# A delta-rule attention and gated-experts kernel: its greedy scheduler against a written order of its steps

## The chip, the cores and the metric

The kernel runs on one core of one Trainium2 chip. The metric is the device time of one launch in microseconds (us). Engines are called by the profile's names: PE (matrix multiply; PEld is its weight load), DVE (vector), ACT (scalar), POOL (GpSimd), SP (the queue that issues the DMAs).

## What is computed

Two layers, one after the other. The first is a recurrent attention over 4 batches, 8 heads, 768 tokens and a head width of 48; the second is a mixture of 4 causal-attention experts over the first one's output, 2 experts per token.

```python
k_n = k / (norm(k) + 1e-06)                    # per token
for t in range(S):                             # S = 768
    y[t]  = q[t] @ state                       # state: 48x48 per batch and head
    state = state + beta[t] * outer(k_n[t], v[t] - k_n[t] @ state)
x = y as (B, S, 384)
logits = x @ w_gate; the top 2 of 4 experts; w = softmax over the two
for e in range(4):                             # width 64
    q, k, v = x @ wq[e], x @ wk[e], x @ wv[e]
    a = softmax(causal(q @ k.T / 8))
    out += gate[e] * (a @ v @ wo[e])
```

## The kernel before

**Tiling.** The work is cut into six units n (NU = 6), each 256 tokens of two batches: units 0, 1, 2 are the three pieces of one pair of batches, 3, 4, 5 of the other, so the state starts anew at unit 3. A unit has four chunks c of 64 tokens (CH = 4). Inside a chunk the recurrence is solved as a triangular system, so that the state moves on chunk by chunk.

**Steps.** All work is cut into small functions; each is one step and has a short name with its indices (unit first). Those that the prediction speaks of:

- lg, lq, lc: loads of k, q and of the k/v pair of a chunk (lines 65, 69, 73), issued on SP; w: load of a weight block, with its split into a high and a low part on ACT and POOL (L130 to L132).
- gr, gq: Gram matrices k.k and k.q of a chunk on PE, brought out of PSUM by ACT (gr, L163; for unit 0 with DVE, L165, L166) or masked by DVE (gq, L175).
- si (L179, L182): three transposes on DVE that lay a unit's Gram matrices out for the solve; pre: the norms (DVE) and the scaling before the solve (L229 on DVE for unit 0, L233 on POOL for the others); sv: the 32 steps of the solve, on DVE for unit 0 (with sg, the other part of the columns, on POOL) and on POOL for units 1 to 5 (L244, L242, L258, L261, L262); so, sn (L278, L275): its result transposed back, on DVE; m1, m2: the halves merged on PE, out by ACT (L290, L304); cl (L311): clears on POOL.
- vt (L78, POOL): v scaled by the norms. ks, u, s, q, y: the chain of a chunk, on PE with ACT (L352, L383, L384) and DVE (L346, L364, L385, L386) between; ks of a chunk needs s of the chunk before it. hx (L392): six small DMAs that spread y for the next layer.
- pj, pv: projections to q, k and v of the experts; gt: gates; mx (L501): scores without exp on PE, maxima over them by DVE; mp, mr: the maxima split and turned to rows; sc: scores again with the maximum taken off, exp on ACT (L552 to L555) ; av: times v, out by ACT (L571, L572); nm, ft, fo (L588, L591, L592, L605, L607): scaling, transposes, the product with wo, and the store.

PE products that leave through the pool `pm_` share three PSUM buffers (gr and gq take two at a time), so a step must wait until the engine behind it has emptied the one three places back. The chunk products and av have PSUM of their own.

**Fillers.** `filler()` is a matmul of zeros with 252 columns into an unused part of the tile po (128x252 in the trace). It computes nothing that is used.

**What sets the order.** Each engine works its instructions off in the order in which the program issues them. The kernel finds this order while it is built, by a greedy scheduler: every step is an `Item` with estimated costs on each engine, dependencies by name, and the PSUM pool that it takes. The items stand in 20 lists; of the heads of the lists whose dependencies are issued, the one with the lowest key goes next, the key being the time at which it can start by the scheduler's own clocks plus a hand-tuned offset by kind and unit (`PRI`). Before a PE step it issues fillers as long as its own clock for PE lies more than 0.355 us before the step's start, and more when its window of matmul columns is low:

```python
if it.pe:
    gap = it.start() - CLK["P"]
    if gap < FMAX:
        while it.start() - CLK["P"] > FMIN:
            CLK["P"] = pe_run(CLK["P"], 0.108, 256)
            filler()
    for _ in range(30):
        if ("gr", 0, CH - 1) not in R or not low(it):
            break
        CLK["P"] = pe_run(CLK["P"], 0.108, 256)
        filler()
it.emit()
```

## Time and profile before

| | us |
|---|---|
| median of 3 runs (570.06 to 574.22) | 572.21 |
| the profiled execution's own time | 573.86 |
| its span, first to last instruction | 572.2 |
| PE busy, fillers included | 520.0 |
| DVE, ACT, POOL busy | 314.1, 260.3, 245.3 |
| mean granted PE clock | 0.981 |

The profile is of one execution. A row of a timeline gives the start in us from the span's start, the duration, the engine, the line, what is written<-read, and how many instructions are merged; in square brackets stands how long the engine had been idle before, and what ended that. A row of groups gives busy time and mean ns of one, then the idle time before the group's instructions. PEclk is the share of the full PE clock that was granted. Matmuls are pipelined, so a row's durations overlap with those of the next.

### The profile page before, as it was taken

What the parts mean: (1) busy time and instruction counts of PE and PEld (TensorE: products, weight loads), DVE (VectorE), ACT (ScalarE), POOL (GpSimd) and SP (SyncE); (2) the same over time, 40 slices, a digit from 0 to 9 for tenths busy, and PEclk for the clock granted to TensorE, in tenths of its full rate; (3) what the DMA queues carried; (4) which work ended last, traced back from release to release, by engine and by line L of the source; (5) the groups of instructions that cost most, each with busy time, mean ns of one, the idle gap of its engine ahead of it and who ended that gap; (6) DMA issues with size and microseconds to landing.
All of it is one profiled execution on the core that took longest, in us unless ns stands there. A gap on an engine that the chain in (4) does not pass through costs nothing. (4 is left out here: it accounts for less than half of the span.)

```text
span 572.2 us, 24003 instructions
## 1 busy us (share of the span) xinstructions
PE 520.0 (91%) x10686; PEld 447.3 (78%) x10686; DVE 314.1 (55%) x745; ACT 260.3 (45%) x642; POOL 245.3 (43%) x422
## 2 busy tenths in 40 slices
PE   6996978888988899898899997999999999999997
PEld 4795767777877668797787886988888787887796
DVE  3996842387534483485888052366744645256701
ACT  2821314335625346357213743574256365574263
POOL 4485266760367811038818875200269810000000
PEclk9997998999999999899899999999999999999999
DMA  8400143200153002520001044002220002110001
GB/s 294 176 11 29 40 118 96 62 1 2 50 181 119 4 1 69 155 71 2 15 15 48 5 122 153 11 1 76 54 67 17 29 3 86 23 37 8 22 2 56
DMA packets 19399, 33.36 MB, mean 58 GB/s; under 512 B 2912, under 2 KB 9440, under 8 KB 19296
## 3 DMA queue, kind: packets, MB, share of 16 engines
q1 hardware_dynamic: 19296, 31.83, 17.9%
q8 instruction: 84, 1.38, 1.0%
q14 instruction: 19, 0.16, 0.1%
HBM read 24.74 MB, written 4.72 MB: 51 GB/s over the span
## 5 line engine op out<-in xcount | busy, mean ns | idle before, releaser
L46 PE MATMUL po<-zb 128*128 128x252 bf16 x798 | 112.8, 281 | 5.7 <-ACT rs L572 3.4
L46 PEld LDWEIGHTS <-zb 128*128 128x128 bf16 x798 | 75.7, 101 | 20.8 <-issue 7.3
L242 POOL TENSOR_TENSOR B<-B,tm 128x30 f32<-128x30 f32 (+9 forms) x150 | 79.0, 527 | 11.7
L244 POOL TENSOR_TENSOR tm<-B 128x30 f32<-128x30 f32 (+9 forms) x150 | 72.7, 485 | 10.4
L78 POOL TENSOR_TENSOR kv<-kv,nt 128x384 f32<-128x384 f32 x24 | 20.3, 848 | 83.9 <-DMA kv<-in_kv_dram 50.6
L46 PE MATMUL po<-VS,at 128*64 128x65 f32 x1344 | 51.1, 229 | 0.3 <-issue 0.3
L46 PEld LDWEIGHTS po<-VS,at 128*64 128x64 f32 x1344 | 44.2, 140 | 5.6 <-issue 2.4
L571 ACT ACTIVATE os<-po 128x128 f32<-128x128 f32 x48 | 13.3, 277 | 44.2 <-PE po L46 44.1
L233 POOL TENSOR_TENSOR B<-B,nn 128x1024 f32<-128x1024 f32 x5 | 11.8, 2366 | 48.1 <-PE pm__4351 L46 18.3
L311 POOL MEMSET tt<- 32x1024 f32 x10 | 9.5, 945 | 53.0 <-PE pm__2438 L46 19.2
L46 PE MATMUL py<-qf,sb 48*48 48x64 f32 x704 | 24.5, 221 | 5.6 <-DVE h L386 5.5
L364 DVE TENSOR_TENSOR sb<-sb,xu 112x384 f32<-112x384 f32 x20 | 11.0, 551 | 30.6 <-PE xu L46 21.7
L46 PEld LDWEIGHTS py<-qf,sb 48*48 48x48 f32 x704 | 21.5, 122 | 8.1 <-DVE h L386 7.3
L383 ACT ACTIVATE xh<-py 112x384 fp32r<-112x384 f32 x24 | 11.8, 490 | 32.9 <-PE py L46 32.1
L385 DVE TENSOR_TENSOR xh<-py,xh 112x384 fp32r<-112x384 f32 x24 | 13.4, 557 | 21.4 <-ACT h L384 21.3
L46 PEld LDWEIGHTS <-identb 128*128 128x128 bf16 x192 | 18.5, 97 | 7.4 <-issue 1.4
L346 DVE TENSOR_TENSOR xs<-kv,xu 128x384 f32<-128x384 f32 x22 | 12.1, 551 | 14.5 <-PE xu L46 10.6
L182 DVE STREAM_TRANSPOSE B<-tt 32x1024 f32<-32x1024 f32 x10 | 19.5, 1954 | 0.2
L46 PE MATMUL xu<-xs,tt 64*64 64x48 f32 x768 | 17.2, 225 | 1.6 <-DVE xs L346 1.5
L519 ACT ACTIVATE mp<-mx 128x8 fp32r<-128x8 f32 x12 | 2.5, 208 | 34.8 <-DVE mx L501 17.9
L46 PE MATMUL xu<-sb,kf 48*64 48x48 f32 x704 | 15.6, 223 | 2.8 <-DVE sb L364 2.0
L46 PEld LDWEIGHTS xu<-sb,kf 48*64 48x64 f32 x704 | 12.7, 134 | 6.6 <-DVE sb L364 4.4
(2005 smaller groups left out, 1461.0 us busy)
## 6 DMA issues: line engine op xcount, KB each, us to landing
kv<-in_kv_dram SPq DMA_DIRECT2D x24, 384.0 KB, 3.7
kf<-in_kq_dram SPq DMA_DIRECT2D x24, 256.0 KB, 3.8
qf<-in_kq_dram SPq DMA_DIRECT2D x24, 256.0 KB, 3.3
out_dram<-ot SPq DMA_DIRECT2D x24, 192.0 KB, 1.9
xh<-h SPq DMA_DIRECT2D x72, 32.0 KB, 2.6
VS<-in_kt_dram SPq DMA_DIRECT2D x4, 192.0 KB, 5.0
wst<-in_wqk_dram SPq DMA_DIRECT2D x3, 256.0 KB, 6.0
wst<-in_wvg_dram SPq DMA_DIRECT2D x1, 256.0 KB, 5.9
```

The lines of the kernel that those rows point to most:

```text
L46: T.matmul(o, lhsT=a, rhs=b, start=start, stop=stop, skip_group_check=True)
L78: G.tensor_tensor(vt, vt, PR[n]["nt"][:, c * NP:c * NP + NP, None].to_broadcast([128, NP, HD]), op=OP.mult)
L182: V.transpose(B[r:r + 32], gf[r:r + 32, :, 0:32].rearrange("p t j -> p j t"))
L233: G.tensor_tensor(B, B, bc(nn, 32), op=OP.mult)
L242: e.tensor_tensor(X[:, a:b, i + 1:], X[:, a:b, i + 1:], tv, op=OP.add)
L244: e.tensor_tensor(tv, R[:, :, i + 1:].to_broadcast([128, w, m]), X[:, a:b, i:i + 1].to_broadcast([128, w, m]), op=OP.mult)
L311: G.memset(TG[n % 2][r + 32:r + 64, :, 0:32], 0.0)
L346: V.tensor_tensor(eight(XB), eight(vt), PX, op=OP.subtract)
L364: V.tensor_tensor(eight(new), eight(state(n, c)), SP, op=OP.add)
L383: S.activation(hi, Y[:, :, 0:3], AF.Copy)
L385: V.tensor_tensor(lo, Y[:, :, 0:3], hi, op=OP.subtract)
L571: S.activation(os[:, :, e], O[:, :, 0:EH], AF.Copy)
```

## The change

The scheduler, its items, costs, clocks and offsets are taken out. In their place stand a string ORDER with the names of all steps in the order in which they are issued, and a table DO from each name to its function. A token like `+41` issues that many fillers at that place.

```diff
+ORDER = """
+fr3 +41 gr0.3 sq0 sr0 sq1 sr1 sq2 +8 gr0.0 sq3 sr2 sr3 lq1.1 pre0.0 +4 gr0.1 lg1.3 pre0.1 pre0.2 pre0.3 lg1.1 kc3 fr1
...
++109 gq0.0 so0 +33 gq0.3 +11 m10.0 w0 sn0 m10.1 +3 m20.0 lg2.0 w5 si1 pre1.0 pre1.1 m20.3 u0.0 pre1.2 pre1.3 w2 m20.2
...
+"""
-    PR = {}
+    PR = {n: dict(gf=TG[n % 2], B=LB[n % 2][:, 1:]) for n in range(NU)}
...
-    CLK = dict(P=0.0, A=0.0, V=0.0, G=0.0)
-    BUF = dict(pm=[0.0] * 3, po=[0.0])
...
+    DO = {}
+    def step(kind, fn, *index):
+        DO[kind + ".".join(map(str, index))] = lambda: fn(*index)
+    for k, a in enumerate(WL):
+        step("w", lambda k: load_weights(*WL[k]), k)
...
+    for x in ORDER.split():
+        if x in DO:
+            DO[x]()
+        else:
+            for _ in range(int(x[1:])):
+                filler()
```

The step functions themselves are the same, and so are the counts of every instruction but the fillers: the program before issues 798 of them (one ahead of the scheduler), the changed one 383. Counted up to four places of the program (in both orders the same names): ahead of u0.0, the first product of the chain, 292 before and 298 now; from there to u1.0 142 and 54; from there to the projections of the last unit (pj5) 321 and 16; behind them 43 and 15. The sets of PE steps that lie between these places are almost the same in both: u0.0 has m20.1 behind it now and gq0.3 and m20.3 ahead of it; u1.0 has av0.1.3 and three of the m21 behind it and q1.0 ahead of it; at pj5 they are equal. What changes is the order inside, and which unit's and which batch's steps alternate. Dependencies that the scheduler took as a whole (mx only when all projections of its unit are done) are now as fine as the data: mx0.0.0.0 stands ahead of the second half's projections.

Three places, as the built programs have them. Lines of the changed program are 61 to 62 higher from the step functions on (L278 is L339 there).

DVE at the end of the first solve, before (L261 and L262 are its last step, L278 is so0, L275 sn0):

```order
L242 TENSOR_TENSOR B_122<-B_122,tm 128x4
L242 TENSOR_TENSOR B_122<-B_122,tm 128x5
L261 TENSOR_TENSOR B_122<-B_122,aa 128x288
L262 COPY B_122<-aa 128x9
L278 STREAM_TRANSPOSE tt_109<-B_122 128x32x32
L275 STREAM_TRANSPOSE tn<-B_122 128x32x32
```

and changed (L236 is the masking of gq):

```order
L303 TENSOR_TENSOR B_122<-B_122,tm 128x4
L303 TENSOR_TENSOR B_122<-B_122,tm 128x5
L322 TENSOR_TENSOR B_122<-B_122,aa 128x288
L323 COPY B_122<-aa 128x9
L236 TENSOR_TENSOR pm<-pm__873,cst 128x256
L236 TENSOR_TENSOR pm<-pm__874,cst 128x256
L339 STREAM_TRANSPOSE tt_109<-B_122 128x32x32
L236 TENSOR_TENSOR pm<-pm__928,cst 128x256
L236 TENSOR_TENSOR pm<-pm__929,cst 128x256
L336 STREAM_TRANSPOSE tn<-B_122 128x32x32
```

Three of the four gq0 steps are done ahead of, or within, so0 and sn0 now (one more pair stands a few rows higher); before they came behind.

DVE at the maxima of unit 2, before (L592 is ft, L179 and L182 are si4, L501 the maxima of batch 0):

```order
L592 TENSOR_TENSOR ol<-pm__4731,oh 128x512
L179 STREAM_TRANSPOSE B_122<-tt_109 128x1024
L182 STREAM_TRANSPOSE B_122<-tt_109 32x1024 x2
L501 TENSOR_REDUCE mx<-pm__4811 128x1
L501 TENSOR_REDUCE mx<-pm__4814 128x1
L501 TENSOR_REDUCE mx<-pm__4817 128x1
L501 TENSOR_REDUCE mx<-pm__4860 128x1
```

and changed (L564 maxima, L582 mp, L593 mr, L511 pv, L240 and L243 si4):

```order
L564 TENSOR_REDUCE mx<-pm__4558 128x1
L582 TENSOR_TENSOR mp<-mx,mp 128x2x4
L236 TENSOR_TENSOR pm<-pm__4566,cst 128x256
L236 TENSOR_TENSOR pm<-pm__4567,cst 128x256
L593 CAST QL<-pm__4586 8x2x256
L564 TENSOR_REDUCE mx<-pm__4593 128x1
L511 COPY lg<-pm__4600 128x4
L240 STREAM_TRANSPOSE B_122<-tt_109 128x1024
L243 STREAM_TRANSPOSE B_122<-tt_109 32x1024 x2
```

The three transposes of si4 stood ahead of the maxima of batch 0; they stand behind them and behind mr2.0 now, where PE goes on with scores that ACT empties.

PE in the last unit, before (three-digit sizes: 128x512 is a full mx product, woh and wol belong to fo):

```order
L46 MATMUL pm__8845<-woh,ol 128x384 x2
L46 MATMUL pm__8855<-KA,QA 128x512
L46 MATMUL pm__8858<-KA,QA 128x512
L46 MATMUL pm__8861<-KA,QA 128x512
L46 MATMUL pm__8864<-KA,QA 128x512
L46 LDWEIGHTS zb
L46 MATMUL po<-zb 128x252
L46 MATMUL pm__8869<-KA,QA 128x128
```

and changed (KA, QA 128x512 is mx; pairs QA, KA and QL, KH are a score):

```order
L109 MATMUL pm__8470<-QL,KH 128x256
L109 MATMUL pm__8476<-KA,QA 128x512
L109 MATMUL pm__8480<-QA,KA 128x256
L109 MATMUL pm__8480<-QL,KH 128x256
L109 MATMUL pm__8480<-QA,KA 128x256
L109 MATMUL pm__8480<-QL,KH 128x256
L109 MATMUL pm__8487<-QA,KA 128x256
L109 MATMUL pm__8487<-QL,KH 128x256
L109 MATMUL pm__8487<-QA,KA 128x256
L109 MATMUL pm__8487<-QL,KH 128x256
L109 MATMUL pm__8493<-KA,QA 128x512
L109 MATMUL po<-VS,at 64x65 x22
```

Where maxima of batch 1 followed one another with fillers between, scores and av of batch 0 stand between them now.

## Prediction

> **What bounds the kernel now.** I read the page first. PE is busy nearly all the time, the other engines about half of it:

> ```profile
> PE 520.0 (91%) x10686; PEld 447.3 (78%) x10686; DVE 314.1 (55%) x745; ACT 260.3 (45%) x642; POOL 245.3 (43%) x422
> PEclk9997998999999999899899999999999999999999
> ```

> But 520.0 us of PE holds the fillers, which compute nothing. So I cut the span at three places that both programs pass in the same state: 63.3 us (u0.0), 149.7 us (u1.0) and 499.7 us (first projection of unit 5). The windows view gives each stretch its length and then PE's busy time:

> ```profile
> 0.00:63.30 63.30, 53.18 (x996) 42.70 (x996) 47.52 (x159) 22.29 (x46) 37.28 (x69) 0.95 0.36 124
> 63.30:149.70 86.40, 75.78 (x1808) 65.02 (x1806) 48.21 (x120) 33.89 (x90) 42.34 (x72) 0.98 0.17 47
> 149.70:499.70 350.00, 323.53 (x7103) 281.00 (x7102) 187.81 (x394) 168.73 (x417) 165.69 (x282) 0.99 0.19 56
> 499.70:572.20 72.50, 67.55 (x786) 58.54 (x783) 30.53 (x73) 35.35 (x91) 0.00 (x0) 0.99 0.08 26
> ```

> and the groups view, asked for the same four windows, the fillers' row in each (count, busy us, mean ns):

> ```profile
> L46 PE MATMUL po<-zb 128*128 128x252 bf16 x292 | 38.7, 297 | 1.1 <-DVE zb L51 1.1
> L46 PE MATMUL po<-zb 128*128 128x252 bf16 x142 | 19.8, 272 | 2.4 <-ACT rs L572 1.8 <-issue 0.6
> L46 PE MATMUL po<-zb 128*128 128x252 bf16 x322 | 47.0, 273 | 1.9 <-ACT rs L572 1.3 <-DVE ol L592 0.4 <-issue 0.2
> L46 PE MATMUL po<-zb 128*128 128x252 bf16 x43 | 7.5, 274 | 0.3 <-ACT rs L572 0.3
> ```

> Busy less fillers is PE's own work: 14.5, 56.0, 276.5 and 60.0 us. The rest of each stretch is lost to PE, by filler or idle: 48.8, 30.4, 73.5 and 12.5 us, 165.2 in all. DVE, the next engine, has 187.8 of 350 us in the longest stretch. So PE's own work and what it waits for between set the time. A filler is not by itself a gain to be had, though: where PE filled while it had to wait, taking the filler out leaves the wait.

> **Stretch 1, up to u0.0.** The first solve on DVE sets it. The timeline of all engines:

> ```profile
> 21.34 1.30 DVE L229 SCALAR_TENSOR_TENSOR B<-B,aa 128x736 f32<-128x736 f32 x2
> 45.43 1.43 POOL L270 TENSOR_TENSOR B<-VS,aa 128x736 f32<-128x736 f32 x1 [1.64 <-DVE B L242]
> 45.52 1.65 DVE L261 TENSOR_TENSOR B<-B,aa 128x288 f32<-128x288 f32 x1
> 48.58 1.95 DVE L278 STREAM_TRANSPOSE tt<-B 128x1024 f32<-128x1024 f32 x1
> 50.44 1.90 DVE L275 STREAM_TRANSPOSE tn<-B 128x1024 f32<-128x1024 f32 x1
> 50.68 1.92 PE L46 MATMUL pm__872<-tt 32*32 32x32 f32 x64 [4.48 <-DVE tt L278]
> 52.53 2.70 PE L46 MATMUL po<-zb 128*128 128x252 bf16 x12
> 55.16 1.44 PE L46 MATMUL pm__919<-tt 32*32 32x32 f32 x64
> 57.26 0.42 DVE L175 TENSOR_TENSOR pm<-pm__955,cst 128x256 f32<-128x256 f32 x1 [4.92 <-PE pm__956 L46]
> 57.93 1.99 DVE L179 STREAM_TRANSPOSE B<-tt 128x1024 f32<-128x1024 f32 x1
> 63.31 0.68 PE L46 MATMUL xu<-xs,tt 64*64 64x48 f32 x32
> ```

> PE has run through all the fillers ahead of m10.0 and stands idle 4.48 us more; the merge begins 0.15 us after so0 has ended (48.58 + 1.95 = 50.53). That end moves by two edits. Two pairs of gq maskings stand ahead of so0 now, each 0.67 us by the start of the next instruction (57.26 to 57.93): +1.4. Ahead of L229 the written order has the Gram matrices as steps of the same kind and count, with fewer fillers between (8, 4, 6 against 6, 6, 12), so that DVE should come to it a little sooner; the trace has no row for that, so I bound it by nothing and by 2 us and take 1. POOL gets a weight split and a vt between its steps, and had 1.64 us to spare at its end; I add nothing.

> From so0 to u0.0 the old order needs 63.31 - 50.53 = 12.8 us: m10.0, 12 fillers, m10.1, two gq with 7 fillers between, m20.0, 12 fillers, m20.1. The new one has m10.0, m10.1, 3 fillers, m20.0, m20.3 and then u0.0, where m20.0 waits for sn0, which is behind one more gq pair: 0.67 + 1.90 = 2.6 us after so0. Behind that come m20.0, its eviction by ACT (0.60 us, the L304 row below) and m20.3. An m2 of unit 0 has 64 products as m10.1 has (1.44 us up to the end of the last); I take 1.2 each, and 5.6 us in all. Sum: 1.4 - 1 + (5.6 - 12.8) = **-6.8 us**, between -9 and -2: u0.0 at 56.5.

> **Stretch 2, u0.0 to u1.0.** One unit alone is in flight, and two chains run: chunk by chunk on PE, ACT and DVE, and the solve of unit 1 on POOL. In time:

> ```profile
> 59.85 0.60 ACT L304 ACTIVATE tt<-pm__1014 128x512 f32<-128x512 f32 x1 [1.05 <-issue]
> 59.96 3.90 DVE L182 STREAM_TRANSPOSE B<-tt 32x1024 f32<-32x1024 f32 x2
> 72.59 2.35 POOL L233 TENSOR_TENSOR B<-B,nn 128x1024 f32<-128x1024 f32 x1 [1.54 <-DVE nn L232]
> 125.59 0.24 POOL L262 COPY B<-aa 128x32 f32<-128x32 f32 x1
> 132.25 1.98 DVE L179 STREAM_TRANSPOSE B<-tt 128x1024 f32<-128x1024 f32 x1 [1.67 <-ACT tt L163]
> 138.17 1.99 DVE L278 STREAM_TRANSPOSE tt<-B 128x1024 f32<-128x1024 f32 x1
> 149.72 0.68 PE L46 MATMUL xu<-xs,tt 64*64 64x48 f32 x32
> ```

> and POOL's groups between 74.9 and 138 us:

> ```profile
> L242 POOL TENSOR_TENSOR B<-B,tm 128x30 f32<-128x30 f32 (+14 forms) x30 | 15.5, 516 | 2.3
> L78 POOL TENSOR_TENSOR kv<-kv,nt 128x384 f32<-128x384 f32 x4 | 3.3, 828 | 9.7 <-DMA kv<-in_kv_dram 4.6 <-DVE h L386 2.8 <-DVE pm L175 1.7
> ```

> The solve takes POOL from 74.9 to 125.8 us, 50.9, of which four vt cost 3.3 and the wait ahead of them 9.7. Then so1 waits another 12.3 us, since si2 stands ahead of it on DVE and itself waits for the last Gram matrix of unit 2. In the new order si1 begins right behind sn0, at about 53.5 instead of 57.9 us, so POOL may start at 70.5; vt1.1 stands behind the solve, and if 3 of the 9.7 us are left, the solve takes 50.9 - 6.7 - 0.8 = 43.4 and ends at 114. The two Gram matrices of unit 2 are issued earlier, so I give so1 4 us behind that, and keep the old 11.6 us from so1 to u1.0: 129.5 against u0.0 at 56.5, a stretch of 73 us. PE alone could do its 56.0 plus 54 fillers of 0.14 us (7.6) in 64. I take 72: **-14 us**, between -22 (PE without a wait) and -3 (si2 as late as before).

> **Stretch 3, u1.0 to the last projections.** 322 fillers become 16. What they cover shows where DVE is kept by a transpose:

> ```profile
> 282.73 3.97 DVE L182 STREAM_TRANSPOSE B<-tt 32x1024 f32<-32x1024 f32 x2
> 285.69 3.83 PE L46 MATMUL po<-zb 128*128 128x252 bf16 x34
> 286.73 0.69 DVE L501 TENSOR_REDUCE mx<-pm__4811 128x1 f32<-128x512 f32 x1
> 396.28 3.91 DVE L182 STREAM_TRANSPOSE B<-tt 32x1024 f32<-32x1024 f32 x2
> 397.57 3.50 PE L46 MATMUL po<-zb 128*128 128x252 bf16 x31
> ```

> Three mx products fill the three PSUM buffers, DVE comes to the first one only when si4 is done at 286.7, and PE fills 3.8 us; the same behind si5. These are waits: without the fillers and in the old order they would stay. The new order puts si4 behind the maxima of its batch and scores (emptied by ACT) behind si4, so PE has work there. Likewise a maximum holds DVE 0.69 us, while its PE product is shorter; rows of maxima that followed each other have scores between them now. Short waits inside the chain (ks, u, s with ACT or DVE between) keep their length, and only more of other units' work between them hides them. Of 73.5 us lost I take half as left, 37; 16 fillers add 2.3 us (47.0 / 322 each). For the clock I add 5 us, three more pieces as below. 276.5 + 37 + 2.3 + 5 = 320.8: **-29 us**. If only the fillers go that cover nothing, it is some -5; if a quarter of the loss is left, -53.

> **The clock.** Fillers also keep PE busy. After the start the trace has four pieces of 3.4 us at half clock. Windows of that length around two of them (third from the end is the granted clock):

> ```profile
> 86.50:89.91 3.41, 1.83 (x62) 1.30 (x62) 0.56 (x1) 0.49 (x1) 1.81 (x4) 1.00 0.23 48
> 89.91:93.33 3.42, 3.30 (x15) 3.31 (x16) 0.76 (x2) 0.28 (x1) 0.19 (x1) 0.50 0.79 264
> 236.69:240.10 3.41, 2.14 (x59) 1.63 (x53) 1.18 (x4) 1.80 (x5) 0.00 (x0) 1.00 0.50 125
> 240.10:243.51 3.41, 3.41 (x112) 3.41 (x111) 3.38 (x2) 0.49 (x1) 0.00 (x0) 0.50 0.74 249
> ```

> A window in which PE was busy 1.83 or 2.14 of 3.41 us was followed by one at half clock, so a piece costs at most half its length, 1.7 us, and comes when some 1.3 us of a window is idle. The new order can have more such windows where a wait is bare now.

> [...]

> **Stretch 4, the end.** 43 fillers become 15, 13 of them at the same place as before, ahead of fo5.1.0:

> ```profile
> 565.21 1.45 PE L46 MATMUL po<-zb 128*128 128x252 bf16 x12
> ```

> That wait for the last ft stays. Of the 12.5 us lost, maxima run beside scores now; I keep 7: **-5.5 us**, between -8 and -1.

> **The sum.** -6.8 - 14 - 29.2 - 5.5 = -55.5 us against the profiled execution's own 573.86 us gives 518.4. Its median stands 1.65 us lower (572.21), so I predict 517 us. All lower bounds together (-9, -22, -53, -8) give 480, all upper ones (-2, -3, -5, -1) 561.

> **Rivals.** (a) The waits stay: the fillers only marked them, and what the new order puts there comes due elsewhere. For it: PE idles 4.48 us at so0 although it filled, and the 34 and 31 fillers above ended with DVE's transpose. Against it: the order puts ready work at just these places. Stretch 1 as forecast, and little else (-6.8, -5, -12, -2; 517 + 30): 547 us. (b) The order fills nearly all: a quarter of the third stretch's loss is left, the others at their lower ends: 480 us, as above. For it: DVE, ACT and POOL are busy only about half of that stretch. (c) Slower, by the clock: without fillers waits are bare, windows fall under the 2.1 us of busy time that the rows show, and PE runs at half clock in many of them; slow work then delays the next chain step and keeps windows thin. PE's own work behind u0.0 is 392.5 us; a share x of it at half clock adds 392.5 x. It decides from x = 0.14 on, where the 55 us won are gone, that is about 32 pieces of 3.4 us against four; at x = 0.19 the time is 517 + 75 = 592 us. Against it: windows at half clock are busy to the brim and are followed by full clock each time. (d) Nothing changes: the written order is in effect the scheduler's, and the fillers only covered waits: 572 us. The three places that the built programs show speak against it.

> **How the numbers follow.** The forecast, 495 to 545 us, has 0.51; (a) 0.20; (b) 0.17; (c) 0.07; (d) 0.05. The range of 477 to 562, the bounds' sums with a little more below, leaves out (c), (d) and under half of (b). About 1% is what a measurement of this kernel can tell from no change. Faster by more than that are the forecast, (a) and (b), 0.88; (d) is within it, 0.05; (c) is slower, 0.07.

> **What would show it.** Right: fillers' busy time falls from 113 to about 55 us, almost all of it ahead of u1.0; u0.0 begins near 57 us and u1.0 near 129; no run of mx behind a bare si4 or si5; PE's own work between the marks unchanged; half-clock pieces fewer than ten behind u0.0. Wrong: u1.0 at 140 us or later (si2 or POOL), PE's idle time in the third stretch above 60 us (rival a), or a mean clock below 0.9 (rival c).

## The result, and the profile after

The changed kernel takes 522.37 us (median of 4 runs, 520.85 to 525.43), the kernel before 573.22 us in the same comparison: a ratio of 0.9136, with a 95% interval of 0.907 to 0.9203. One of the four runs of the kernel before, 579.78 us, was a slow one and does not count in the ratio. The profiled execution of the changed kernel took 521.83 us with a span of 520.0; the prediction had 517 us for the median. The page, and the windows cut at the same places:

```profile
PE 465.0 (89%) x10271; PEld 408.9 (79%) x10271; DVE 320.4 (62%) x745; ACT 261.1 (50%) x642; POOL 245.9 (47%) x422
...
PEclk9898999979899999999979999999899998999999
```

```profile
0.00:58.06 58.06, 50.69 (x1035) 41.71 (x1035) 48.34 (x163) 20.73 (x43) 32.71 (x65) 0.94 0.37 128
58.06:132.62 74.56, 63.05 (x1615) 54.38 (x1611) 50.31 (x112) 33.03 (x88) 46.37 (x76) 0.95 0.21 63
132.62:449.97 317.35, 288.21 (x6874) 256.67 (x6873) 191.20 (x399) 171.53 (x423) 166.81 (x282) 0.97 0.20 61
449.97:520.03 70.06, 63.09 (x758) 56.13 (x756) 30.57 (x72) 35.80 (x91) 0.00 (x0) 0.99 0.08 27
```

and the fillers' groups in these four windows:

```profile
L109 PE MATMUL po<-zb 128*128 128x252 bf16 x298 | 37.6, 287 | 1.1 <-DVE zb L114 1.1
L109 PE MATMUL po<-zb 128*128 128x252 bf16 x54 | 9.3, 294 | 0.4 <-ACT rs L634 0.4
L109 PE MATMUL po<-zb 128*128 128x252 bf16 x17 | 3.2, 273 | 0.9 <-ACT rs L634 0.9
L109 PE MATMUL po<-zb 128*128 128x252 bf16 x15 | 2.1, 272 | 0.0
```

Busy time less fillers is PE's own work: 13.1, 53.8, 285.0 and 61.0 us. What is left of each stretch, filler and idle together, is 45.0, 20.8, 32.3 and 9.0 us: 107.1 instead of 165.2. Stretch by stretch the change is -5.2, -11.8, -32.6 and -2.4 us; the prediction had -6.8, -14, -29 and -5.5. Most of the gain is the third stretch, as forecast. (A filler's row begins before the row of the product ahead of it has ended, in the kernel before for example at 285.69 against 285.86 us. So "busy less fillers" is too low where there are hundreds of them, by an estimated 4 us in the third stretch before, as the first experiment shows.)

Of the three wrong-if conditions none came: u1.0 stands at 132.6, PE idles 29.1 us in the third stretch, and the mean clock is 0.97. Of the signs of being right, most came: the fillers' busy time is 52.2 us, 46.9 of it ahead of u1.0; u0.0 is at 58.1; five pieces behind u0.0 ran at half clock. Two did not come as put: behind si4 a product of the maxima waits bare for 2.77 us, and PE's own work in the third stretch reads 8.5 us more than before.

### The profile page after: what moved, and what is told of

Its sections match the earlier page's. It is cut to its first block, busy times and chain, and to the rows that moved or that the text cites. A ratio compares the mean times of both kernels' runs of the same rounds, so it can differ in the third digit from the quotient of the medians.

```text
span 520.0 us, 23164 instructions
## 1 busy us (share of the span) xinstructions
PE 465.0 (89%) x10271; PEld 408.9 (79%) x10271; DVE 320.4 (62%) x745; ACT 261.1 (50%) x642; POOL 245.9 (47%) x422
## 4 chain that ended last, share of the span: by engine, by line
PE 68%; DVE 15%; ACT 9%; issue 6%; DMA 1%; SPq 0%; ACTq 0%; DVEq 0%
PE po L109 13%; PE xu L109 7%; PE py L109 6%; DVE tm L305 2%; DVE B L303 2%; ACT QA L486 2%; ACT QA L483 1%; DVE mx L564 1%; ACT KH L489 1%; ACT KA L483 1%; DVE QL L494 1%; DVE KA L492 1%; DVE B L243 1%; DVE B L240 1%; ACT VS L510 1%
## 5 line engine op out<-in xcount | busy, mean ns | idle before, releaser
L305 POOL TENSOR_TENSOR tm<-B 128x30 f32<-128x30 f32 (+9 forms) x150 | 74.3, 495 | 10.9
L109 PE MATMUL po<-zb 128*128 128x252 bf16 x383 | 51.9, 287 | 2.5 <-ACT rs L634 1.3
L141 POOL TENSOR_TENSOR kv<-kv,nt 128x384 f32<-128x384 f32 x24 | 19.9, 830 | 60.9 <-DMA kv<-in_kv_dram 48.6
L109 PEld LDWEIGHTS <-zb 128*128 128x128 bf16 x383 | 37.7, 103 | 8.8 <-DVE zb L114 1.1
L446 ACT ACTIVATE xh<-py 112x384 fp32r<-112x384 f32 x24 | 11.8, 492 | 28.4 <-PE py L109 28.4
L109 PE MATMUL py<-pm,ub 64*48 64x64 f32 x768 | 18.0, 228 | 5.2 <-issue 5.0
L243 DVE STREAM_TRANSPOSE B<-tt 32x1024 f32<-32x1024 f32 x10 | 19.9, 1994 | 0.2
L109 PE MATMUL xu<-sb,kf 48*64 48x48 f32 x704 | 16.8, 229 | 3.6 <-issue 3.2
L109 PEld LDWEIGHTS py<-pm,ub 64*48 64x48 f32 x768 | 14.6, 129 | 6.1 <-issue 5.6
L109 PE MATMUL xu<-xs,tt 64*64 64x48 f32 x768 | 18.5, 227 | 0.8 <-issue 0.7
```

The lines of the kernel that those rows point to most:

```text
L109: T.matmul(o, lhsT=a, rhs=b, start=start, stop=stop, skip_group_check=True)
L141: G.tensor_tensor(vt, vt, PR[n]["nt"][:, c * NP:c * NP + NP, None].to_broadcast([128, NP, HD]), op=OP.mult)
L243: V.transpose(B[r:r + 32], gf[r:r + 32, :, 0:32].rearrange("p t j -> p j t"))
L305: e.tensor_tensor(tv, R[:, :, i + 1:].to_broadcast([128, w, m]), X[:, a:b, i:i + 1].to_broadcast([128, w, m]), op=OP.mult)
L446: S.activation(hi, Y[:, :, 0:3], AF.Copy)
```

## The experiments

Each experiment is the changed program with another list of steps; line numbers differ by one or two where the list has more or fewer lines. Stretches 1 to 4 are those of the profiled execution; "half" is the time behind u0.0 in which its clock record shows half clock, without a last piece that begins when PE has nothing more to do. The diffs show excerpts of the lists, broken into lines anew. The kernels were timed in several sessions, in which the kernel before had medians of 570.35 to 573.22 us; the ratios are against the one of the same session, so differences of a few us between rows are to be read from the ratios and their intervals. The stretches are of one execution each.

| kernel | time, us | ratio to before, 95% | stretches 1, 2, 3, 4 | half, us |
|---|---|---|---|---|
| before | 573.22 | | 63.3, 86.4, 350.0, 72.5 | 13.7 |
| changed | 522.37 | 0.907 to 0.920 | 58.1, 74.6, 317.4, 70.1 | 23.9 |
| e1 old order, bare | 578.02 | 1.005 to 1.021 | 63.0, 84.7, 357.0, 70.8 | 68.3 |
| e2 new order, refilled | 541.30 | 0.942 to 0.956 | 60.2, 75.8, 335.4, 70.0 | 20.5 |
| e3 front old | 533.17 | 0.925 to 0.945 | 59.8, 87.8, 312.1, 69.8 | 20.5 |
| e4 tail old | 523.01 | 0.911 to 0.924 | 58.4, 75.8, 317.2, 72.5 | 23.9 |
| e5 si4 back | 526.57 | 0.917 to 0.928 | 59.3, 72.0, 323.2, 70.1 | 30.7 |
| e6 maxima in runs | 533.85 | 0.932 to 0.942 | 58.8, 71.7, 327.1, 72.1 | 23.9 |
| e7 no late fillers | 529.51 | 0.926 to 0.934 | 59.6, 84.8, 312.5, 69.5 | 64.9 |
| e8 so1 first | 524.84 | 0.916 to 0.926 | 57.7, 70.3, 322.0, 70.3 | 23.9 |
| e9 waits filled | 518.16 | 0.903 to 0.917 | 58.8, 72.4, 310.6, 70.1 | 6.8 |
| e10 second stretch | 531.78 | 0.924 to 0.937 | 58.6, 75.9, 323.2, 70.0 | 51.2 |
| e11 pre4 behind | 518.66 | 0.902 to 0.913 | 58.5, 72.1, 313.8, 71.7 | 13.7 |
| e12 both | 515.53 | 0.900 to 0.908 | 56.5, 72.3, 312.7, 70.0 | 6.8 |

My theory was that the order brings the gain, by putting ready work where PE waited, and that the old fillers mostly marked these waits. The main rival was that 415 fillers fewer, at 0.14 to 0.17 us each, are the gain. A second rival was the clock.

**Old order without fillers behind u1.0** (the scheduler's own order, written out, 365 fillers left out):

```diff
-mx2.0.0.0 mx2.0.0.1 mx2.0.0.2 sv3.17 sv3.18 sv3.19 +34 mx2.0.0.3 +1 mx2.0.0.4 +1 mx2.0.0.5
+mx2.0.0.0 mx2.0.0.1 mx2.0.0.2 sv3.17 sv3.18 sv3.19 mx2.0.0.3 mx2.0.0.4 mx2.0.0.5
```

> The old order, written out as a list, with its fillers up to u1.0 kept and the 365 fillers behind u1.0 left out. If the gain comes from the order (the fillers only marked waits, which stay as bare waits), the third stretch stays within 330 to 348 us of its 350 and the kernel takes 552 to 570 us. If it comes from not issuing fillers (322 of 0.146 us = 47 us in the third stretch, 43 of 0.17 = 7.5 in the fourth), it takes 518 to 530 us and the third stretch about 303 to 310. If bare waits bring the half clock (rival c), over ten half-clock windows behind u1.0 and 575 us or more.

It took 578.02 us, slower than before (570.35 us in the same session). Its third and fourth stretch:

```profile
147.66:504.63 356.97, 308.06 (x6785) 269.56 (x6781) 187.50 (x394) 169.23 (x417) 165.96 (x282) 0.91 0.18 55
504.63:575.43 70.80, 64.15 (x743) 54.96 (x741) 30.53 (x73) 35.38 (x91) 0.00 (x0) 0.99 0.08 26
```

Without a single filler the third stretch is 7.0 us longer. Idle time is 48.9 us, so by estimate 20 to 25 of the 73.5 us lost before had covered nothing. But PE's own work takes 308.1 instead of 276.5 us: the clock record has eight pieces at half clock there, 64.8 us together, instead of 10.2. Half of that difference, 27.3 us, is most of the 31.6; the other 4.3 I put down to the overlap of the fillers' rows. The filler theory is out by some 50 us. Mine was right that the waits stay, and wrong by 9 us in the length, because I left the clock nearly where it was. What came is the third outcome that I had named, over ten windows at half clock and more than 575 us: rival (c)'s mechanism, in the old order.

**New order with the old fillers put back** (each of 322 ahead of the step that it stood ahead of, between u1.0 and pj5):

```diff
-sv3.13 sv3.14 mx2.0.0.3 pj2.1.2 mx2.0.1.9 pv2.1.1 av1.1.2 +1 mx2.0.1.10 mx2.0.1.7
+sv3.13 sv3.14 +34 mx2.0.0.3 pj2.1.2 mx2.0.1.9 pv2.1.1 av1.1.2 +2 mx2.0.1.10 +1 mx2.0.1.7
```

> The new order, with the old order's fillers between u1.0 and pj5 put back ahead of the same steps that they stood ahead of (322 more). They cover nothing there now, unless a wait is still at the same step. Order theory: most of them is new work on PE, 25 to 47 us more than the changed kernel, 547 to 570 us, and those of them that stand at steps that still wait cost nothing. If fillers keep the clock up so that PE gains by them, under 20 us more. Filler theory: the same 45 us or more, and then the first kernel of this call at 520 to 530 tells the two apart.

It took 541.30 us, 19 more than the changed kernel. The third stretch and its fillers:

```profile
135.96:471.36 335.40, 318.05 (x7194) 281.21 (x7194) 187.18 (x399) 171.98 (x423) 167.25 (x282) 0.98 0.19 58
```

```profile
L111 PE MATMUL po<-zb 128*128 128x252 bf16 x338 | 49.3, 273 | 3.7 <-ACT rs L636 2.0 <-issue 1.7
```

49.3 us of fillers lengthened the stretch by 18.0: idle time fell to 17.4 us, and half clock from 17.1 to 10.2 us. This was under the 25 us that I expected, and is the outcome that I had tied to the clock. The two runs with before and changed give a square for the third stretch:

| | old fillers | without (16 left in the new order) |
|---|---|---|
| old order | 350.0 | 357.0 |
| new order | 335.4 | 317.4 |

The order alone is worth 14.6 us with the fillers left in. Taking the fillers out costs 7.0 us in the old order and brings 18.0 in the new one. Neither theory has this: the gain is the two together, since of these two only the denser order can do without its fillers.

**Front and tail.** The old order up to u1.0 and the new one behind it. The kernel has 13 of the 31 fillers behind u1.0, not all as I had meant: the 16 of the third stretch and two of the fourth are out.

```diff
-fr3 +41 gr0.3 sq0 sr0 sq1 sr1 sq2 +8 gr0.0
+lg1.0 lg1.1 lg1.2 lg1.3 lq1.0 lq1.1 lc0.1 +8 gr0.0 sq0 sq1 sr0 +6 gr0.1
```

> The old order with its fillers up to u1.0, then the new order for all steps that are left, with its 31 fillers. By the sum of stretches (5.2 + 11.8 us of the gain lie ahead of u1.0) it takes 17 us more than the changed kernel, 536 to 542 us, with the third stretch at 315 to 321 us. If the new third stretch lives on what the new front has prepared (transfers, solve of unit 2 begun), it is longer than 325 and the kernel above 545.

Then the new order up to pj5.0.0 and the old one behind it:

```diff
-pj5.0.0 pj5.0.2 hx5.3.0 mx5.0.0.1 pj5.1.0 mx5.1.0.3 pj5.1.2 mx5.0.0.5
+hx5.3.0 pj5.0.2 pj5.0.0 pj5.1.2 pj5.1.0 fo4.0.0 av4.1.2 fo4.0.1 +1 mx5.0.0.0 mx5.0.0.1 mx5.0.0.2 +2 mx5.0.0.3
```

> The new order up to pj5.0.0, then the old order of the last unit with its 43 fillers. By the sum of stretches 2.5 us more than the changed kernel, 523 to 526 us, with a fourth stretch of 72 to 73 us. If the gain of the fourth stretch was handed on by the third, no difference (within 1 us).

The old front costs 10.8 us by the medians (533.17), where the stretches of the two profiles had promised 17: its first two stretches are 14.9 us longer than the changed kernel's, and its third is 5.3 us shorter. Some 2.4 us of that are steps (av0.1.3 and three m21) that the old front has already done at u1.0. The rest, 3 us, is about what the fillers that it lacks took in the changed kernel (3.2 us); that they are the reason fits with 312.5 us in the run without late fillers below, but no run leaves out these alone. The old tail makes the fourth stretch 72.5 instead of 70.1 us, 2.4 as expected, though the medians show only 0.6 and the ratios 2.3, which is within what they tell apart. In the bare old order that stretch has 70.8 us, so 1.7 of the 2.4 us would be its fillers and 0.7 the order; profiles with the new order there lie between 70.0 and 71.7 us, so the 0.7 is not shown.

**One transposition moved back.** In the new order si4 stands behind mr2.0; here it goes ahead of the last six maxima of batch 0:

```diff
-gr4.2 sv3.16 mx2.0.0.0 +2 mx2.0.0.5
+gr4.2 si4 pre4.0 sv3.16 mx2.0.0.0 +2 mx2.0.0.5
...
-fo1.0.1 si4 pre4.0 sv3.23
+fo1.0.1 sv3.23
```

> The changed kernel with one move: si4 (three transposes of DVE, 5.9 us together) and pre4.0 go back from behind mr2.0 to directly behind gr4.2, ahead of the last six maxima of batch 0, as they stood in the old order. Theory of the order (a transposition ahead of maxima is a wait of PE, behind mr it has scores under it): a bare wait of 3 to 4 us at the third maximum behind si4, and 2 to 5 us more in all. Rival (the wait only moves, since in the changed kernel PE waits 2.77 us behind si4 too and at half clock for 6.8 us after it): the time within 1.5 us, with the 2.77 us gone.

The timeline of DVE and PE at that place:

```profile
250.56 1.94 DVE L240 STREAM_TRANSPOSE B<-tt 128x1024 f32<-128x1024 f32 x1 [0.79 <-ACT tt L224]
252.53 3.85 DVE L243 STREAM_TRANSPOSE B<-tt 32x1024 f32<-32x1024 f32 x2
...
257.11 0.68 DVE L564 TENSOR_REDUCE mx<-pm__4545 128x1 f32<-128x512 f32 x1
...
257.85 0.79 PE L109 MATMUL pm__4570<-KA,QA 128*128 128x512 f32 x1 [6.58 <-DVE mx L564]
```

The fourth product behind si4 waits 6.58 us, for all of si4 and the first steps of pre4.0, not 3 to 4 as I had it: only three PSUM buffers stand between PE and DVE. 10.2 us at half clock go with it. The old place of this wait (2.77 us ahead of mx2.1.0.0) is gone. In all it is 4.2 us more by the medians, 5.8 by the third stretch; the intervals of the two kernels overlap, so the size is not settled. The wait itself is shown: the place of one instruction group matters as the prediction said, and twice, once as a wait and once by the clock.

**Maxima in runs.** In units 1 to 5 the maxima of batch 1 that stand between the scores of batch 0 go behind these, as one run:

```diff
-sc5.0.0.0 sc5.0.1.1 mx5.1.1.9 av5.0.0 mx5.1.1.7 mx5.1.0.4 sc5.0.1.2 sc5.0.2.0 mx5.1.0.2 mx5.1.0.1 mx5.1.0.6 av5.0.1
+sc5.0.0.0 sc5.0.1.1 av5.0.0 sc5.0.1.2 sc5.0.2.0 av5.0.1
```

> The changed kernel, but in units 1 to 5 the maxima of batch 1 that stand between the scores of batch 0 are put together in one run behind these (5, 13, 2, 7 and 12 of them), as they mostly were in the old order. If the gain of the third and fourth stretch comes from such interleaving, DVE's 0.69 us for each sets these runs while PE needs about 0.5: 39 x 0.19 = 7 us, less three buffers at each run, and more where a thin run brings the half clock: 4 to 15 us more than the changed kernel. If it comes from elsewhere (transposes, front, fillers), within 2 us.

It took 533.85 us, 11.5 more than the changed kernel; the third stretch is 9.7 us longer (327.1) and the fourth 2.0 (72.1). The third:

```profile
130.48:457.56 327.08, 291.76 (x6873) 259.28 (x6873) 188.52 (x399) 171.25 (x423) 166.92 (x282) 0.96 0.19 59
```

So some 12 of the 35 us that the third and fourth stretch won come from this one pattern. How it works is only argued: a maximum holds DVE 0.69 us, and a score, which ACT empties, gives PE something to do meanwhile. Of the 9.7 us, 6.2 are more idle time of PE (35.3 instead of 29.1 us), but the waits put down to the maxima grew by only 0.9 us, the others being spread over many places; the rest is own work, with 23.9 instead of 17.1 us at half clock.

**No fillers behind u0.0**, all 85 left out:

```diff
-sv1.21 sv1.22 +12 mx0.0.1.2
+sv1.21 sv1.22 mx0.0.1.2
```

> The changed kernel without its 85 fillers behind u0.0 (54 in the second stretch, 31 behind it). Theory that they still keep the clock, as the bare old order suggests (64.8 us at half clock in its third stretch instead of 10.2): more half-clock windows in the second stretch, 2 to 8 us more than the changed kernel. Theory that they only cost (85 of 0.17 us, of which some lie under waits): 2 to 6 us less.

529.51 us, 7.1 more, the outcome of the first theory. Its second stretch is 84.8 us long, at a granted clock of 0.73. Windows of 3.41 us, from the wait ahead of mx0.0.1.2 on:

```profile
108.30:111.71 3.41, 0.64 (x6) 0.43 (x4) 2.69 (x7) 3.31 (x6) 2.94 (x7) 1.00 0.00 0
111.71:115.12 3.41, 2.65 (x11) 2.09 (x12) 2.61 (x4) 0.00 (x0) 2.86 (x8) 0.50 0.00 0
115.12:118.53 3.41, 3.03 (x43) 2.30 (x42) 2.15 (x5) 1.18 (x5) 3.02 (x6) 0.50 0.00 0
...
135.60:139.01 3.41, 2.90 (x66) 2.58 (x68) 0.54 (x3) 0.70 (x5) 0.00 (x0) 0.50 0.20 70
...
152.67:156.08 3.41, 3.41 (x94) 3.17 (x94) 2.20 (x5) 1.09 (x2) 2.37 (x5) 0.50 0.15 53
156.08:159.49 3.41, 3.13 (x176) 2.84 (x174) 1.18 (x3) 1.42 (x6) 0.00 (x0) 1.00 0.52 111
```

Behind one window with PE busy 0.64 us the granted clock is at half from 111.7 us on, and it stays there for thirteen windows, 44.4 us, although PE is busy 2.65 to 3.42 of each 3.41 us. The 54 fillers of the second stretch, 9.3 us of PE time, are worth 10.3 us of the stretch. The third and fourth stretch, which lost the other 31, are 4.9 and 0.6 us shorter than in the changed kernel, at about as much half clock (18.5 us against 17.1 in the third). So only the fillers of the second stretch are seen to pay; a kernel without the other 31 alone was not run.

**so1 ahead of si2**, with m11 and m21.0 ahead of the last scores of unit 0. In the changed kernel POOL ends the solve at 115.9 us and DVE does si2 first. The timelines of DVE and POOL there:

```profile
115.61 1.97 DVE L240 STREAM_TRANSPOSE B<-tt 128x1024 f32<-128x1024 f32 x1
117.61 3.94 DVE L243 STREAM_TRANSPOSE B<-tt 32x1024 f32<-32x1024 f32 x2
121.58 2.01 DVE L339 STREAM_TRANSPOSE tt<-B 128x1024 f32<-128x1024 f32 x1
...
115.67 0.24 POOL L323 COPY B<-aa 128x32 f32<-128x32 f32 x1
```

```diff
-av0.1.2 av0.0.2 si2 sc0.0.1.0 so1 sn1 av0.1.1 pre2.0 av0.1.0 sc0.0.3.0 vt1.1 sc0.0.0.0 q1.0 av0.0.3 av0.0.1
-pre2.1 pre2.2 pre2.3 pre2.4 +1 av0.0.0 m11.0 m11.1 cl1 +6 m21.0 nm0.0 pre2.5 sc0.1.3.0 +5 u1.0
+av0.1.2 so1 sn1 m11.0 av0.0.2 m11.1 cl1 vt1.1 si2 sc0.0.1.0 av0.1.1 m21.0 sc0.0.3.0 av0.1.0 q1.0 u1.0 sc0.0.0.0 pre2.0 av0.0.3
```

> The changed kernel with so1 and sn1 ahead of si2 on DVE, m11 and m21.0 ahead of the last scores of unit 0, and without the 12 fillers between av0.0.1 and u1.0. In the changed kernel POOL's solve is done at 115.9 us, and so1 begins at 121.6, behind si2. If si2 ahead of so1 is what sets u1.0 (as the prediction's second step says of the old order), u1.0 comes 5 to 9 us earlier, and the whole time falls by 2 to 4 us, since the scores moved behind u1.0 have to be done there. If u1.0 was set by PE's own work, u1.0 moves but the time stays within 1 us.

u1.0 comes 4.6 us earlier, at 128.0. That does not show that si2 had set the mark, because the edit also takes scores and 12 fillers away from ahead of u1.0. The rows of PE speak against it. In the changed kernel so1 ended at 123.59, and m11.0, which reads its result, began 3.8 us later and without a wait, behind scores, av and a filler:

```profile
119.35 0.57 PE L109 MATMUL po<-VS,at 128*64 128x65 f32 x12 [0.44 <-ACT rs L634]
...
127.37 1.20 PE L109 MATMUL pm__2331<-tt 32*32 32x32 f32 x64
...
132.62 0.80 PE L109 MATMUL xu<-xs,tt 64*64 64x48 f32 x32
```

From 118 us to u1.0 PE never idled longer than the 0.44 us at a time shown, so PE's own queue set m11.0 there, and with it u1.0. With so1 first m11.0 does wait for it:

```profile
117.34 1.20 PE L109 MATMUL pm__2207<-tt 32*32 32x32 f32 x64 [1.44 <-DVE tt L339]
```

The time is not better (524.84 us, 0.916 to 0.926): the third stretch takes the 4.6 us back, which is the second outcome, PE's own work. That work moved behind the mark, and a new wait came with my edit:

```profile
137.50 2.34 POOL L294 TENSOR_TENSOR B<-B,nn 128x1024 f32<-128x1024 f32 x1 [14.36 <-DVE rs L638]
...
137.76 2.09 DVE L640 TENSOR_TENSOR rs<-rs,gates 128x8 f32<-128x8 f32 x1
...
140.72 1.09 PE L650 MATMUL pm__2551<-cst,os 128*128 128x128 f32 x4 [4.11 <-DVE os L641]
```

A second try at this stretch also put nm0.0 ahead of the pre2 steps, gt0 behind mr0.0, and the two pv0.1 in the place of the 12 fillers:

```diff
-pv0.1.0 pv0.1.1 gt0 pj0.1.0 pj0.1.2 sv1.21 sv1.22 +12 mx0.0.1.2
+pj0.1.0 pj0.1.2 pv0.1.0 pv0.1.1 sv1.21 sv1.22 mx0.0.1.2
```

> The changed kernel with the second stretch mended: gt0 (13 steps of DVE, 4.5 us) behind mr0.0 instead of ahead of the evictions of pj0.1, the two pv0.1 behind pj0.1.2 in place of the 12 fillers, so1 and sn1 ahead of si2 as in the run before, and nm0.0 ahead of pre2.1 to pre2.5. If what is left in this stretch are waits behind DVE (2.23 us ahead of mx0.0.1.2 and its 6.8 us at half clock; 4.11 us ahead of ft0.0 in the run with so1 first), u1.0 is at 122 to 127 us and the whole 3 to 7 us shorter than the changed kernel. If PE's own work moved behind u1.0 takes it all back, within 1.5 us.

It missed: 531.78 us. u1.0 is at 134.5, with 20.3 us of the second stretch at half clock instead of 6.8. The longer of its two pieces lasted 27.3 us, from 121.0 on and into the third stretch; PE had waited 2.25 us bare for so1 until 120.55. The stretch lacks 24 of its fillers and went to half clock as in e7, so whether the order by itself would have been better stays open.

**The clock alone: 84 fillers more**, all where PE waits bare in the changed kernel:

```diff
-+12 mx0.0.1.2
++27 mx0.0.1.2
...
-pv2.0.0 sc2.0.1.0 av2.0.0 mx2.1.0.0
+pv2.0.0 sc2.0.1.0 av2.0.0 +18 mx2.1.0.0
```

> The changed kernel with 84 fillers more, all at places where its PE waits bare: 15 ahead of mx0.0.1.2, 18 ahead of mx2.1.0.0, 7 to 10 ahead of pj2.1.0, mx1.1.0.2, mx4.0.1.7, pj5.1.0, gq4.2 and av2.1.0. If thin windows bring the half clock and fillers prevent it at no cost where PE waits anyway, the pieces at 109.6, 266.6 and 369 us (13.7 us together in the changed kernel, 6.8 us at most of lost time) are gone and the time is 2 to 6 us less. If fillers delay what they stand ahead of, 1 to 6 us more.

**pre4.0 behind the evictions that hold PSUM.** DVE, POOL and PE in the changed kernel behind si4:

```profile
258.59 4.09 DVE L243 STREAM_TRANSPOSE B<-tt 32x1024 f32<-32x1024 f32 x2
262.72 1.72 DVE L265 COPY ss<-B 128x32 f32<-128x32 f32 x1
...
262.48 1.91 POOL L322 TENSOR_TENSOR B<-B,aa 128x1024 f32<-128x1024 f32 x1
...
265.40 0.68 DVE L654 TENSOR_TENSOR ol<-pm__4678,oh 128x512 fp32r<-128x512 f32 x1
...
266.14 0.50 PE L109 MATMUL pm__4732<-KA,QA 128*128 128x512 f32 x1 [2.77 <-DVE ol L654]
```

```diff
-si4 pre4.0 sv3.23 sc2.0.0.2 fo1.0.0 sv3.24 sv3.25 sv3.26 ft1.1 pv2.0.0 sc2.0.1.0
+si4 sv3.23 sc2.0.0.2 fo1.0.0 sv3.24 sv3.25 sv3.26 ft1.1 pv2.0.0 pre4.0 sc2.0.1.0
```

> The changed kernel with pre4.0 (2.77 us of DVE behind si4) moved behind the evictions of ft1.1 and pv2.0.0, which hold the PSUM buffers that mx2.1.0.0 waits for. If that wait (2.77 us) hangs on DVE's order, it falls to about 0.3 us, the 6.8 us at half clock behind it go too, and the third stretch is 3 to 6 us shorter than 317.3. If the solve of unit 4, which starts behind pre4.0, is what the rest waits for, no gain.

By the medians both gained, with 518.16 and 518.66 us, but their intervals (0.903 to 0.917 and 0.902 to 0.913) overlap that of the changed kernel, so neither gain alone is clear of noise. The windows view of the third stretch, first with the waits filled:

```profile
131.24:441.84 310.60, 290.68 (x6934) 258.10 (x6933) 189.03 (x399) 171.35 (x423) 167.43 (x282) 0.99 0.21 62
```

then with pre4.0 moved:

```profile
130.56:444.32 313.76, 284.99 (x6873) 253.75 (x6873) 188.22 (x399) 171.44 (x423) 167.38 (x282) 0.98 0.20 62
```

With the waits filled the stretch has 10.7 us of fillers and 19.9 of idle time, 30.6 lost instead of 32.3, but own work of 280.0 instead of 285.0 us: half clock fell from 17.1 to 6.8 us, and half of that difference is the 5 us. In this profile the fillers cost nothing where they stood, and paid by the clock. With pre4.0 moved the wait of 2.77 us fell to 0.10, yet 32.0 us are lost as before (others grew, 1.25 us ahead of sc2.0.1.1 among them); the 3.6 us won are, but for 0.2, half of the 6.9 us less at half clock.

**Both together**, and 3 instead of 11 fillers ahead of m10.0:

```diff
-+33 gq0.3 +11 m10.0
++33 gq0.3 +3 m10.0
```

> The two gains of the call before together: the changed kernel with pre4.0 behind pv2.0.0, fillers at the bare waits (15 ahead of mx0.0.1.2, 9, 7, 7, 9, 9 and 10 ahead of pj2.1.0, mx1.1.0.2, mx4.0.1.7, pj5.1.0, gq4.2 and av2.1.0, 7 ahead of sc2.0.1.1, and only 3 ahead of mx2.1.0.0, whose wait is gone), and 3 instead of 11 fillers ahead of m10.0 (1.1 us past the end of so0 in the changed kernel). If both hold, under 1.5 half-clock pieces of 6.8 us behind u0.0, u0.0 1 us earlier, and 511 to 517 us, a ratio under 0.905. If the two gains are one (both only remove the half clock behind mx2.1.0.0), 517 to 520 us.

515.53 us (median of 6), ratio 0.9039, 0.8995 to 0.9084: the fastest version by the medians, 7 us or 1% under the changed kernel, whose interval it overlaps by 0.001. u0.0 is at 56.45, 1.6 us earlier. Against either one alone it is 2.6 and 3.1 us faster by the medians, which their intervals don't separate.

## Why the prediction was right, point by point

**The bound and the waits.** Right: fillers are not by themselves a gain. It was truer than I put it: in the old order taking them out loses 7 us of the third stretch.

**Stretch 1** (-6.8 predicted, -5.2 in the profiles). so0 ended at 51.55 instead of 50.9, and the merge did not begin there:

```profile
49.59 1.96 DVE L339 STREAM_TRANSPOSE tt<-B 128x1024 f32<-128x1024 f32 x1
...
51.38 1.36 PE L109 MATMUL po<-zb 128*128 128x252 bf16 x11
...
52.67 1.09 PEld L109 LDWEIGHTS pm__959<-tt 32*32 32x32 f32 x64 [0.21 <-issue]
```

I had m10.0 wait for so0 only; gq0.3 and 11 fillers stand between and kept PE 1.1 us longer. With 3 of them u0.0 was at 56.45, the predicted 56.5, but that is partly luck: the solve of that execution also began 1.0 us earlier (19.11 instead of 20.08).

so0 itself was late by a term that I put at nothing. From the scaling ahead of the solve (L229 before, L290 changed) to so0 it took 29.5 us instead of 27.2, and the two pairs of gq are 1.3 of these 2.3. A step of the solve, first before, then changed, with POOL's weight split beside it:

```profile
24.96 0.38 DVE L242 TENSOR_TENSOR B<-B,tm 128x52 f32<-128x52 f32 x2
...
24.13 1.59 DVE L303 TENSOR_TENSOR B<-B,tm 128x52 f32<-128x52 f32 x2
...
24.09 1.27 POOL L195 TENSOR_TENSOR wvgl<-wst,wvgh 128x512 fp32r<-128x512 f32 x1
```

I had asked only whether POOL has the time for its weight split and its vt; here the split holds a DVE step up by 1.2 us. The 1 us that I took off for fewer fillers between the Gram matrices rests on a misreading, since the old list has 6, 6 and 6 there, as many as the new one; that L290 came 1.3 us earlier is luck, as it begins anywhere from 19.1 to 22.0 us in the profiles with the new front.

The size is also uncertain in itself: ten profiles with the new front have u0.0 between 57.7 and 60.2 us, three with the old one between 59.8 and 63.3. The lowest of these three, e3, has the same order there as the kernel before, but its m10.0 ran at full clock (1.20 instead of 1.92 us), where the kernel before had half clock from 49.0 to 55.8 us. So a part of the 5.2 us is the clock, not the order.

**Stretch 2** (-14 predicted, -11.8). The solve ended at 115.9 instead of 114, and si2 cost so1 5.7 us instead of 4. But this chain, which I added up to u1.0, is not what ended last: m11.0 began 3.8 us behind so1 without having waited for it, and PE's own queue set the mark (the rows stand with e8). In the kernel before it was 2.5 us in the same way (140.16 to 142.70), so the 11.6 us that I kept from so1 to u1.0 held 2.5 us of PE's own queue, fillers included. That is the step of the prediction that failed: the path through si2 and so1. The length came near all the same, which is luck as far as the path goes. Of five profiles with this same part of the list, three have 71.7 to 72.1 us with no half clock in it, as I took, the changed kernel 74.6 with 6.8 us at half clock and e4 75.8 with 10.2.

**Stretch 3** (-29 predicted, -32.6). Of 73.5 us lost I kept 37 and 2.3 of fillers; 32.3 are lost, fillers included, 7 less than I kept. Own work was to rise by the 5 us for the clock; it reads 8.5 more, of which 3.4 are the clock and some 4 the overlap of the old fillers' rows. These errors partly cancel, and that half of the loss stays was a guess with no row behind it, so that the sum is only 3.5 us off is in part luck. The two reasons given were tested one by one: si4 behind the maxima is worth 4 to 6 us, not clear of noise, and the alternation of maxima and scores 12 with the tail's part. The third piece, that fillers leave, brings 18 us in this order. The wait behind si4 that I took to be covered was not: pre4.0 follows si4 on DVE and kept two PSUM buffers.

**The clock** (5 us added). This term was about right in size: 17.1 us at half instead of 10.2 is 3.4 us. Its reasoning failed in one step: I wrote that windows at half clock are busy to the brim and followed by full clock each time, and held rival (c) for unlikely on that. That was so for the four pieces that I counted; I had left out a fifth, ahead of u0.0, of two windows (49.0 to 55.8 us), with PE busy 1.73 us in the first. Pieces of 10 to 44 us do come where fillers are left out (e1, e7, e10), and of 10.2 us in e5, which keeps them all. The written order is not safe from it by its density alone; the 54 fillers that it keeps in the second stretch hold off 40 us at half clock there (46.4 in e7 against 6.8).

**Stretch 4** (-5.5 predicted, -2.4). This is the term that was most off in proportion: 9.0 us stay lost, not 7, and own work reads 1.0 more. The 13 fillers ahead of fo5.1.0 stand as before. Fillers fell from 7.5 to 2.1 us, but idle time rose from 5.0 to 7.0: the new order brought waits for DVE's evictions, 1.59 us ahead of pj5.1.0 (456.31) and 0.88 ahead of a product of the maxima (462.69), where the longest bare wait before was 0.35 us.

**Rivals.** (a) is out: its third stretch was 338, 20 us off. (b) would have needed a quarter of the loss left; 44% are (32.3 of 73.5). (c) did not come in this order, whose mean clock is 0.97. (d) is out.

## What to carry to other kernels

A filler in a wait cost nothing that could be seen here (30.6 us of the third stretch lost in e9, 32.3 in the changed kernel), and fillers in front of ready work did (18 us for 322 in e2): which it is depends on the order around it, so order and fillers have to be changed and timed together. Taking fillers out of an order that still waits can be slower than leaving them (578.02 us in e1, 570.35 before). When a list of steps is written by hand, look for the steps behind a long one on the same engine that hold another engine's buffers, and put those first: in e11 that took a wait from 2.77 to 0.10 us. And before a path is added up to a mark, look whether the last engine on it waits for that path at all, or is still busy with other work.

## What the hardware showed that was not expected

| PE busy in the window, us | at full clock: windows, of them next at half | at half clock: windows, of them next at half |
|---|---|---|
| under 1.5 | 39, 39 | 4, 4 |
| 1.5 to 1.75 | 17, 13 | 2, 2 |
| 1.75 to 2.0 | 43, 15 | 1, 1 |
| 2.0 to 2.5 | 153, 13 | 4, 4 |
| 2.5 to 3.0 | 379, 4 | 10, 10 |
| 3.0 to 3.3 | 306, 1 | 12, 10 |
| over 3.3 | 1039, 0 | 104, 25 |

At full clock a window with a third of it idle mostly kept its clock (140 of the 153 with PE busy 2.0 to 2.5 us); at half clock only 2 of the 33 windows with PE busy up to 3.3 us were followed by full clock, and of the fuller ones a quarter were not. Behind the bare 2.77 us in the dense third stretch of the changed kernel two windows ran at half clock, 3.4 us lost at most; behind the window of e7 with PE busy 0.64 us, with small waits following, thirteen did, 22 us at most. No bare wait behind u0.0 in the changed kernel was longer than 2.77 us, and it had seven windows at half clock.

**Some small DVE instructions waited for a POOL instruction that was running.** The copy at the head of pre1 to pre5 (128x32) took 0.14 to 0.19 us in 19 of 25 cases in five traces (before, changed, e9, e11, e12). In the other six a POOL instruction was running when it started, and it took 0.53 to 1.72 us: the 1.72 us above end at 264.44 us, POOL's TENSOR_TENSOR of 128x1024 began at 262.48 and ended at 264.39. All six end 0.03 to 0.05 us behind POOL's end. L640 in e8 is of the same kind (2.09 instead of 0.17 us, in the rows above), and so is the step of the first solve that POOL's weight split held up. Not every DVE instruction was held like this. In the changed kernel L529 ran inside POOL's L141 and took its usual 0.22 us:

```profile
193.91 0.83 POOL L141 TENSOR_TENSOR kv<-kv,nt 128x384 f32<-128x384 f32 x1
...
194.08 0.22 DVE L529 TENSOR_REDUCE grk<-gc 128x16 f32<-128x64 f32 x1
```

What I had not expected is the size of such a wait: one, on the engine whose eviction PE waits for, held DVE up by about 1.5 us, more than half of the 2.77 us of the longest wait left in the third stretch.
